# Letting the second expert's search into the last rows, and transposing the next expert's rows after the sixth chunk

## The chip, the cores and the metric

One core of a Trainium2 chip runs the whole program. The metric is the device time of one execution in microseconds (us); the figure quoted is the median over several executions. Engines are named as in the profile: PE (matrix multiply, PEld its weight loads), DVE (VectorE), ACT (ScalarE), POOL (GpSimd), SP (SyncE, which issues most transfers).

## The reference: what is computed

Three layers in a row, all in float32. A gated linear attention (4 batches, 8 heads, 768 steps, head size 48) makes 3072 tokens of 384 numbers. A dense two-layer network with 2048 hidden units follows. Then a mixture of 8 experts, each with room for exactly 3072/8 = 384 tokens, assigned greedily:

```
order = np.argsort(-flat)              # all 3072 x 8 logits, largest first
for idx in order:
    tok, e = int(idx) // E, int(idx) % E
    if assigned[tok] >= 0 or counts[e] >= cap: continue
    assigned[tok] = e
    counts[e] += 1
...
for e in range(E):
    h = np.maximum(x[assigned == e] @ w1[e], 0.0)      # 384 -> 1024
    out[assigned == e] = h @ w2[e]                     # 1024 -> 384
```

## The kernel before, in words

**Stages.** The tokens are worked in eight blocks of 384. Attention and the dense network run block by block; meanwhile the weights of all experts are split into a high and a low part and stored to the DRAM tensor `wd`. For the last block the dense network is done in two steps: `ffn1_logits` first makes its hidden layer and the gate logits, and `ffn1_rows` (144 matmuls on `hidden`, in three groups of 128 tokens) then makes the rows themselves, which in the text are called the last rows. The experts follow; they are numbered 0 to 7 here in the order in which they are filled, not by their weights.

**One expert.** `expert(p)` has eight chunks of hidden units. `hidden(f)` is nine matmuls 128x384 (three products of high and low parts, three slices of the input), then a Relu on ACT and a subtraction on DVE that split the result in two. `project(f)` is nine matmuls for the second layer. `project` lags `hidden` by two chunks, so PE's order is h0 h1 h2 p0 h3 p1 ... h7 p5 p6 p7, 144 matmuls for an expert. In the trace and the order, `weights` is a weight tile and `rounded` a split operand; positions such as "matmul 81 of expert 2" count these 144.

**What an expert needs.** Its token list comes from `chain(p)` and `lists`. `chain(p)` finds which expert fills up next and at which logit: four search steps in `seek`, each a comparison on DVE (`late<-late,cols` 128x1536), twelve counting matmuls (`bank<-late` 128x16) and a few small ones (`late,pairs`, `ok`), then `take`. `lists` turns the result into row numbers (24 matmuls `bank<-late` 128x6 and short DVE work). `gather` then issues three indirect DMAs on POOL that fetch 128 rows of `x2d` each (`common<-x2d`), and `expert_x` transposes each 128x384 piece with three matmuls against the identity (`bank<-ident,common`) and splits the result (ACT and DVE). The results of an expert go out by three indirect DMAs on POOL (`put`, `out_dram<-common`). Weights come in eight transfers of 768 KB on SP's queue (`weights<-wd`), issued when the chain knows which expert it is.

**For expert 0** there is a shortcut, `first_x`: two pieces are gathered and transposed as above. The third is built from the gathered rows, and from the last rows directly by matmuls with picking matrices (`late,common`), since the last rows are not yet in DRAM.

**What sets the order.** The program is not emitted as written. `Plan` records every instruction with its dependences, a modelled cost and a priority number, and `schedule` then walks through modelled time: at each step the instruction that can start earliest is taken, and among equals the one with the lowest priority number. The order of each engine is fixed by that; on the chip an engine that finds its next instruction not ready waits. `at(x)` sets the priority, `behind(ops)` says that what is recorded inside may not start before `ops` have started. Where the planner sees PE idle it puts in filler matmuls (`bank<-ones` 128x512, line 1711). The priorities that matter here: the last rows have ROWS = 84, the chain of expert 1 has CHAIN1 = 99 (line 57), and for expert p the base is 100 + 10p, with the lists, gather and transposes of expert p+1 at base - 1.5, the chain of p+2 at base - 1 and the expert's own matmuls at base + 5. Two experts ahead the chain runs, one expert ahead the rows are fetched.

Of the kernel before, what the change touches and what calls it, by code (L numbers as in the profile page):

```python
# [21 lines left out]
E, FE = 8, 1024  # L22
# [31 lines left out]
CHAIN0 = 81.0  # L54
GATHER0 = 80.9
ROWS = 84
CHAIN1 = 99
LISTS = -1.5
CHAIN = -1
EXPERT = 5.0  # L60
# [574 lines left out]
class Kernel:  # L635
# [860 lines left out]
    def expert(self, p, idx, x):  # L1496
        nc = self.nc
        ws = self.expert_tiles(p)
        w1, w2 = ws[:4], ws[4:]
        po = [self.pp.tile([128, 512], F32, name="x", bufs=BT) for _ in range(3)]  # L1500
        G = {}

        def hidden(f):
            ph = self.pp.tile([128, 512], F32, name="h", bufs=2)
            n = 0
            for s, v in ((1, x[0]), (0, x[1]), (0, x[0])):
                for kd in range(KD):

                    u, at = divmod(kd * 256 + f % 2 * 128, DM)
                    nc.tensor.matmul(ph[:, :CAP], w1[f // 2][:, u, s, at:at + 128], v[:, kd, :], start=(n == 0), stop=(n == 3 * KD - 1))  # L1510
                    n += 1
            G[f] = hH, hL = self.pair(f)
            with self.at(self.urgent):
                nc.scalar.activation(hH, ph[:, :CAP], AF.Relu)
                nc.vector.scalar_tensor_tensor(hL, ph[:, :CAP], 0.0, hH.bitcast(F32), op0=OP.max, op1=OP.subtract)

        def project(f, t):
            hH, hL = G[f]
            ts = slice(t * 128, (t + 1) * 128)
            for n, (h, s) in enumerate(((hL, 0), (hH, 1), (hH, 0))):  # L1520
                nc.tensor.matmul(po[t][:, :DM], h[:, ts], w2[f // 2][:, f % 2, s, :], start=(f == 0 and n == 0), stop=(f == NFE - 1 and n == 2))

        def put(t):
            o = self.gw.tile([128, DM], F32, name="x2", bufs=3)
            nc.scalar.activation(o, po[t][:, :DM], AF.Copy)
            nc.gpsimd.indirect_dma_start(out=self.out, out_offset=bass.IndirectOffsetOnAxis(ap=idx[:, t:t + 1], axis=0),
                                         in_=o, in_offset=None)

        if self.plan and p == E - 1:
            for f in range(NFE):  # L1530
                hidden(f)
            for t in range(3):
                for f in range(NFE):
                    project(f, t)
                put(t)
            return
        LAG = LAG2
        for f in range(NFE + LAG):
            if f < NFE:
                hidden(f)  # L1540
            if f >= LAG:
                for t in range(3):
                    project(f - LAG, t)
        for t in range(3):
            put(t)
# [172 lines left out]
    def record(self, cp):  # L1718
# [16 lines left out]
        def chain(p):  # L1735
            if p == 0:
                self.choose(NT - BT, NT)
                self.begin(NT - BT, NT)
                self.first(NT - BT, NT)
            else:  # L1740
                self.choose()
            if 0 < p < E - 1:
                self.begin()
                self.first()
            if p < E - 1:
                self.seek(p)
            else:
                self.take(p, None, None, None, None)
                self.flag()
            return self.pos, self.acc, self.ei  # L1750
# [55 lines left out]
        with self.at(CHAIN0):  # L1806
            c = chain(0)
            self.expert_weights(0, c[2], slice(0, AHEAD))
            idx, tok = self.lists(*c[:2], first=True)
# [3 lines left out]
        with self.at(GATHER0):  # L1813
            xg = self.gather(idx, NE + 1)
# [3 lines left out]
            ready = tok, self.first_x(xg, rows)  # L1818
# [3 lines left out]
        self.plan.extra = 3500.0  # L1822
        with self.at(CHAIN1), self.behind(listed):
            nxt = chain(1)
            self.expert_weights(1, nxt[2])
        for p in range(E):
            base = 100.0 + 10 * p
            self.urgent = base + XURG
            cur, was = ready, nxt
            if p + 2 < E:  # L1830
                with self.at(base + CHAIN):
                    nxt = chain(p + 2)
            if p + 1 < E:
                with self.at(base + LISTS):
                    idx, tok = self.lists(*was[:2])
                    ready = tok, self.expert_x(self.gather(idx))
            self.wide = p == E - 1
            with self.at(base + EXPERT):
                self.expert(p, *cur)
            if p + 2 < E:  # L1840
                with self.at(base + CHAIN):
                    self.expert_weights(p + 2, nxt[2])
# [49 lines left out]
```

## Time and profile before

| | |
|---|---|
| device time, median of 3 runs | 846.14 us (842.1 to 849.03) |
| the profiled execution | 847.83 us |
| its span, first to last instruction | 846.1 us |
| PE busy | 814.3 us (96%) |
| DVE busy | 567.0 us (67%) |
| ACT, POOL busy | 347.8 us (41%), 112.2 us (13%) |
| mean granted clock of PE | 0.990 |

The busy shares are means over the whole span. A PE that is busy 96% says that little is left, not where it is: the idle time has to be looked up by what PE waited for. In the timeline the duration of a matmul (0.34 us) is longer than the distance to the next one, because matmuls overlap; what a matmul costs is the distance between starts.

### The profile page before, as it was taken

To read this page: it belongs to the slowest core of one execution; us is meant where nothing else is said; L and a number is where in the kernel's file an instruction comes from. 1 tells how busy PE (TensorE), PEld (TensorE's weight loads), DVE (VectorE), ACT (ScalarE), POOL (GpSimd) and SP (SyncE) were. 2 spreads that over 40 slices of the span, in tenths; PEclk is the share of its full clock that TensorE was granted. 3 is DMA by queue.
4 is the path that set the end of the run, shared out by engine and by line. 5 is a ranking of instruction groups with operands and counts; after the bars stand their busy time and mean duration, and the time that the engine had idled before them with its cause. 6 is when DMAs were issued, how large, how long until landed. Compare 5 with 4: busy or idle time off the path is not lost. (4 is left out here: it accounts for less than half of the span.)

```text
span 846.1 us, 16045 instructions
## 1 busy us (share of the span) xinstructions
PE 814.3 (96%) x6116; PEld 751.5 (89%) x6116; DVE 567.0 (67%) x1329; ACT 347.8 (41%) x742; POOL 112.2 (13%) x107
## 2 busy tenths in 40 slices
PE   7999989999999999999999999999999899999995
PEld 3688888999999999998999999888887789899995
DVE  6899977977956966966976754655766667452220
ACT  3576765355555455455455443511121222222230
POOL 3111101200200200300200000001021212311211
PEclk7999999999999999999999999999999999999998
DMA  7894203689879688888879760003867866687400
GB/s 178 260 299 115 48 20 84 138 287 295 237 267 288 150 282 257 239 271 275 247 240 305 251 225 29 1 10 117 334 260 316 324 259 237 245 315 245 150 28 32
DMA packets 92935, 172.60 MB, mean 204 GB/s; under 512 B 31818, under 2 KB 61522, under 8 KB 92850
## 3 DMA queue, kind: packets, MB, share of 16 engines
q1 hardware_dynamic: 89634, 162.04, 59.1%
q0 software_dynamic: 3072, 9.44, 3.1%
q8 instruction: 50, 0.82, 0.4%
q14 instruction: 35, 0.29, 0.1%
q10 hardware_dynamic: 144, 0.01, 0.0%
HBM read 111.69 MB, written 59.77 MB: 203 GB/s over the span
## 5 line engine op out<-in xcount | busy, mean ns | idle before, releaser
L213 PE MATMUL bank<-rounded,weights 128*128 128x384 f32 (+1 forms) x1740 | 352.5, 343 | 1.2 <-POOL weights L213 0.5
L213 PE MATMUL bank<-weights,rounded 128*128 128x392 f32 (+1 forms) x1620 | 326.4, 343 | 3.3 <-ACT weights L213 2.4
L213 PEld LDWEIGHTS bank<-rounded,weights 128*128 128x128 f32 (+1 forms) x1740 | 301.9, 187 | 8.0 <-issue 2.6
L213 PEld LDWEIGHTS bank<-weights,rounded 128*128 128x128 f32 x1620 | 284.8, 188 | 5.9 <-issue 3.3
L213 ACT ACTIVATE rounded<-bank 128x384 fp32r<-128x384 f32 x110 | 53.8, 491 | 211.2 <-PE bank L213 190.4
L213 DVE TENSOR_TENSOR early<-early 128x384 fp32r<-128x384 f32 (+2 forms) x196 | 120.2, 628 | 21.5 <-ACT early L213 20.5
L213 PEld LDWEIGHTS bank<-early 128*64 128x64 f32 (+2 forms) x1696 | 98.2, 153 | 20.4 <-issue 10.2
L213 ACT ACTIVATE early<-early 128x384 fp32r<-128x384 f32 (+2 forms) x177 | 95.5, 547 | 41.8 <-DMA wd<-early 27.4
L213 PE MATMUL bank<-early 128*64 128x128 f32 (+3 forms) x1696 | 110.1, 269 | 2.2 <-ACT early L213 1.2
L213 POOL TENSOR_TENSOR rounded<-common,rounded 128x384 fp32r<-128x384 f32 x36 | 48.3, 1342 | 433.8 <-ACT rounded L213 394.6
L213 DVE SCALAR_TENSOR_TENSOR common<-common,rest,bank 128x384 f32<-128x384 f32 x128 | 77.9, 608 | 41.6 <-ACT common L233 40.9
L213 ACT ACTIVATE rounded<-common 128x384 fp32r<-128x384 f32 x118 | 61.7, 523 | 65.8 <-DVE common L213 62.4
L233 ACT ACTIVATE common<-bank 128x384 f32<-128x384 f32 x128 | 62.0, 485 | 61.7 <-PE bank L213 61.5
L213 DVE SCALAR_TENSOR_TENSOR rounded<-bank,rounded 128x384 fp32r<-128x384 f32 x62 | 34.4, 555 | 49.6 <-ACT rounded L213 47.6
L213 DVE TENSOR_TENSOR rounded<-common,rounded 128x384 fp32r<-128x384 f32 x82 | 46.4, 566 | 28.1 <-ACT rounded L213 19.6
L213 DVE TENSOR_TENSOR_SCAN early<-early 128x516 f32<-128x516 f32 x48 | 62.7, 1305 | 1.7 <-ACT early L213 1.3
L213 ACT ACTIVATE common<-bank 128x384 f32<-128x384 f32 x48 | 23.1, 490 | 59.1 <-PE bank L213 58.2
L213 POOL DMA_INDIRECT out_dram<-common,late x24 | 24.2, 1010 | 155.2 <-ACT common L213 100.5
L213 DVE TENSOR_TENSOR late<-late,cols 128x1536 bf16<-128x1536 bf16 (+3 forms) x53 | 42.7, 816 | 0.2
L213 POOL DMA_INDIRECT common<-x2d,late x24 | 26.2, 1092 | 103.3 <-DVE late L213 52.0
L213 DVE TENSOR_TENSOR rounded<-bank,rounded 128x384 fp32r<-128x384 f32 x48 | 26.6, 555 | 14.0 <-ACT rounded L213 13.1
L213 DVE TENSOR_TENSOR early<-bank,mask 128x512 f32<-128x512 f32 x48 | 31.0, 683 | 2.8 <-PE bank L213 2.4
(114 smaller groups left out, 485.6 us busy)
## 6 DMA issues: line engine op xcount, KB each, us to landing
wd<-early SPq DMA_DIRECT2D x128, 384.0 KB
weights<-wd SPq DMA_DIRECT2D x64, 768.0 KB
early<-in_w_dram SPq DMA_DIRECT2D x64, 384.0 KB
early<-in_fkq_dram SPq DMA_DIRECT2D x46, 288.0 KB
raw<-in_w_in_dram SPq DMA_DIRECT2D x16, 384.0 KB
raw<-in_w_out_dram SPq DMA_DIRECT2D x16, 384.0 KB
early<-in_v_dram SPq DMA_DIRECT2D x24, 192.0 KB
x2d<-common SPq DMA_DIRECT2D x24, 192.0 KB
```

What stands on the lines that cost most here:

```text
L213: op = self.add(engines, lambda e, b: getattr(e, method)(*[b(x) for x in a], **{n: b(x) for n, x in k.items()}), outs, ins)
L233: return e.activation(b(out), b(x), AF.Relu, scale=-1.0)
```

## The change

Two edits. CHAIN1 goes from 99 to 82, below ROWS = 84, so instructions of the chain of expert 1 that are ready are taken ahead of the last rows' matmuls. And `expert_x` for expert p+1, which was recorded together with its gather ahead of `expert(p)`, is recorded behind `expert(p)` with the condition that it may not start before the last matmul of `hidden(5)`, the sixth chunk, has started. The gather stays where it was.

```diff
--- before.py
+++ after.py
@@ -54,7 +54,8 @@
 CHAIN0 = 81.0
 GATHER0 = 80.9
 ROWS = 84
-CHAIN1 = 99
+CHAIN1 = 82
+MID = 5
 LISTS = -1.5
 CHAIN = -1
 EXPERT = 5.0
@@ -1509,6 +1510,8 @@
                     u, at = divmod(kd * 256 + f % 2 * 128, DM)
                     nc.tensor.matmul(ph[:, :CAP], w1[f // 2][:, u, s, at:at + 128], v[:, kd, :], start=(n == 0), stop=(n == 3 * KD - 1))
                     n += 1
+            if f == MID:
+                self.middle = self.last(1)
             G[f] = hH, hL = self.pair(f)
             with self.at(self.urgent):
                 nc.scalar.activation(hH, ph[:, :CAP], AF.Relu)
@@ -1833,10 +1836,13 @@
             if p + 1 < E:
                 with self.at(base + LISTS):
                     idx, tok = self.lists(*was[:2])
-                    ready = tok, self.expert_x(self.gather(idx))
+                    xg = self.gather(idx)
             self.wide = p == E - 1
             with self.at(base + EXPERT):
                 self.expert(p, *cur)
+            if p + 1 < E:
+                with self.at(base + LISTS), self.behind(self.middle):
+                    ready = tok, self.expert_x(xg)
             if p + 2 < E:
                 with self.at(base + CHAIN):
                     self.expert_weights(p + 2, nxt[2])
```

Three places show what the planner makes of it. (Lines behind 82 stand one to six lines later in the changed file, so L213 is L214 there.)

PE at the end of the last rows. `weights_...,hidden` are the last rows' matmuls, `ident,common` the transposes of expert 0's rows. Before:

```order
L213 MATMUL bank_69<-weights_1154,hidden 128x384 x6
L213 MATMUL bank_69<-weights_1235,hidden 128x384 x4
L213 MATMUL bank_66<-ident,common 128x128 x3
L213 MATMUL bank_69<-weights_1235,hidden 128x384 x2
L213 MATMUL bank_69<-weights_1322,hidden 128x384 x2
L213 MATMUL bank_67<-ident,common 128x128 x3
L213 MATMUL bank_69<-weights_1322,hidden 128x384 x4
L213 MATMUL bank_68<-ident,common 128x128 x3
```

Now (the row of "..." is eleven more counting steps of two rows each):

```order
L214 MATMUL bank_69<-weights_1154,hidden 128x384 x5
L214 LDWEIGHTS late
L214 MATMUL bank_66<-late 128x16
...
L214 MATMUL bank_69<-weights_1154,hidden 128x384
L214 MATMUL bank_69<-weights_1235,hidden 128x384 x2
L214 MATMUL bank_67<-ident,common 128x128 x3
L214 MATMUL bank_66<-late,pairs 128x8
L214 MATMUL bank_69<-weights_1235,hidden 128x384 x3
L214 MATMUL bank_66<-ident,common 128x128 x3
L214 MATMUL bank_69<-weights_1235,hidden 128x384
```

The first search step of expert 1 (twelve counting matmuls) and its `late,pairs` now stand between the last rows' matmuls; before, they came behind the last of them.

PE in expert 2, where the rows of expert 3 are transposed. `rounded,weights` is `hidden`, `weights,rounded` is `project`. Before (the "..." is one search step, counting matmuls):

```order
L213 MATMUL bank_71<-weights_1012,rounded 128x384 x3
L213 MATMUL bank_66<-ident,common 128x128 x3
L213 LDWEIGHTS ones
L213 MATMUL bank_68<-ok_83,ones 128x1
L213 MATMUL bank_69<-weights_1012,rounded 128x384 x3
L213 MATMUL bank_67<-ident,common 128x128 x3
L213 MATMUL bank_72<-rounded,weights_687 128x384 x4
...
L213 MATMUL bank_72<-rounded,weights_687 128x384 x4
L213 MATMUL bank_66<-ident,common 128x128 x3
```

Now:

```order
L214 MATMUL bank_69<-weights_1095,rounded 128x384 x3
L214 MATMUL bank_73<-rounded,weights_687 128x384 x9
L214 MATMUL bank_66<-ident,common 128x128 x3
L214 MATMUL bank_68<-ident,common 128x128 x3
L214 MATMUL bank_67<-ident,common 128x128 x3
L214 MATMUL bank_70<-weights_1095,rounded 128x384 x3
L214 MATMUL bank_71<-weights_1095,rounded 128x384 x3
L214 MATMUL bank_69<-weights_1095,rounded 128x384 x3
L214 MATMUL bank_72<-rounded,weights_862 128x384 x9
```

The three transposes of three matmuls stood at matmuls 51, 54 and 62 of the expert; now all nine stand behind matmul 81, which is the end of `hidden(5)`.

POOL from the gathers of experts 0 and 1 on (six, in the first row); `out_dram` are the stores of results. Before:

```order
L213 DMA common<-x2d,late 128x384 x6
L213 DMA out_dram<-common,late 3072x384 x2
L213 DMA common<-x2d,late 128x384
L213 DMA out_dram<-common,late 3072x384
L213 DMA common<-x2d,late 128x384 x2
L213 DMA out_dram<-common,late 3072x384
L213 DMA common<-x2d,late 128x384 x2
L213 DMA out_dram<-common,late 3072x384
```

Now:

```order
L214 DMA common<-x2d,late 128x384 x6
L214 DMA out_dram<-common,late 3072x384 x2
L214 DMA common<-x2d,late 128x384 x3
L214 DMA out_dram<-common,late 3072x384 x2
L214 DMA common<-x2d,late 128x384 x3
L214 DMA out_dram<-common,late 3072x384 x3
```

The three gathers of an expert now stand together; before, stores of results stood between those of experts 2 and 3.

## Rows read from the trace of the kernel before

**Rows 1.** The page, parts 1 and 2: PE's busy time, and the granted clock by slices.
```profile
PE 814.3 (96%) x6116; PEld 751.5 (89%) x6116; DVE 567.0 (67%) x1329; ACT 347.8 (41%) x742; POOL 112.2 (13%) x107
...
PEclk7999999999999999999999999999999999999998
```

**Rows 2.** The waits of PE: us in total, times, longest.
```profile
PE bank L213 <- DMA common<-x2d,late: 6.4, 9, 2.2
...
PE bank L213 <- DVE late L213: 1.1, 4, 0.4
```

**Rows 3.** The timeline of PE, transposes that waited: start, us, what, [idle before <-releaser].
```profile
622.41 0.55 PE L213 MATMUL bank<-ident,common 128*128 128x128 f32 x3 [0.18 <-DMA common<-x2d,late]
...
623.99 0.52 PE L213 MATMUL bank<-ident,common 128*128 128x128 f32 x3 [0.33 <-DMA common<-x2d,late]
...
650.10 0.55 PE L213 MATMUL bank<-ident,common 128*128 128x128 f32 x3 [1.61 <-DMA common<-x2d,late]
...
671.49 0.55 PE L213 MATMUL bank<-ident,common 128*128 128x128 f32 x3 [0.45 <-DMA common<-x2d,late]
...
677.39 0.52 PE L213 MATMUL bank<-ident,common 128*128 128x128 f32 x3 [2.22 <-DMA common<-x2d,late]
...
705.62 0.52 PE L213 MATMUL bank<-ident,common 128*128 128x128 f32 x3 [0.16 <-DMA common<-x2d,late]
...
768.07 0.55 PE L213 MATMUL bank<-ident,common 128*128 128x128 f32 x3 [0.65 <-DMA common<-x2d,late]
```

**Rows 4.** The timeline of POOL: gathers (common<-x2d) and row stores (out_dram<-common).
```profile
582.84 1.12 POOL L213 DMA_INDIRECT common<-x2d,late  x1 [51.98 <-DVE late L213]
...
637.60 0.99 POOL L213 DMA_INDIRECT common<-x2d,late  x1 [8.75 <-issue]
638.89 0.98 POOL L213 DMA_INDIRECT out_dram<-common,late  x1 [0.30 <-issue]
...
641.47 0.96 POOL L213 DMA_INDIRECT common<-x2d,late  x1 [0.30 <-PE bank L213]
...
668.92 0.99 POOL L213 DMA_INDIRECT out_dram<-common,late  x1 [2.08 <-DMA out_dram<-common,late]
670.22 0.97 POOL L213 DMA_INDIRECT common<-x2d,late  x1 [0.30 <-PE bank L213]
```

**Rows 5.** The timeline of PE where the last rows end and expert 0 begins.
```profile
586.11 0.55 PE L213 MATMUL bank<-ident,common 128*128 128x128 f32 x3 [0.17 <-DMA common<-x2d,late]
...
588.04 0.52 PE L213 MATMUL bank<-ident,common 128*128 128x128 f32 x3 [0.68 <-DMA common<-x2d,late]
...
589.28 0.94 PE L213 MATMUL bank<-ident,common 128*128 128x128 f32 x6
...
591.11 0.59 PE L1711 MATMUL bank<-ones 128*128 128x512 bf16 x2
591.65 1.15 PE L213 MATMUL bank<-rounded,weights 128*128 128x384 f32 x5
```

**Rows 6.** The timeline of PE: what a matmul and a search step cost.
```profile
595.10 0.46 PE L213 MATMUL bank<-late 128*128 128x16 bf16 x12
595.42 0.95 PE L213 MATMUL bank<-rounded,weights 128*128 128x384 f32 x4
...
635.72 0.36 PE L213 MATMUL bank<-late 128*128 128x6 bf16 x8
...
779.72 4.91 PE L213 MATMUL bank<-weights,rounded 128*128 128x384 f32 x27
784.47 0.76 PE L213 MATMUL bank<-late 128*128 128x6 bf16 x24
```

**Rows 7.** Windows: length, busy us of the engines, PEclk, DMA share, GB/s.
```profile
10.00:20.00 10.00, 8.10 (x48) 5.15 (x49) 7.26 (x19) 3.94 (x8) 0.00 (x0) 0.54 0.88 225
...
582.00:589.00 7.00, 6.15 (x37) 5.47 (x35) 3.41 (x10) 0.90 (x2) 3.56 (x3) 1.00 0.38 117
...
634.00:650.00 16.00, 14.13 (x130) 11.97 (x128) 11.14 (x37) 2.84 (x6) 3.92 (x4) 1.00 1.01 401
```

## The prediction

> **What bounds the kernel now.** I read the page first. PE is busy for 814 of 846 us and its granted clock is full in every slice but the first and the last [rows 1]. So PE sets the time, and a change can win only what PE spends waiting, or lose by new waits; no matmul of the reference's work goes away. Next the waits of PE by releaser. Two kinds fall into the part that the change touches: 6.4 us in nine waits for a gather from `x2d`, and 1.1 us in four waits for DVE's search work [rows 2]. That is 7.5 us, or 0.9% of the time, and an upper bound for what new places can win. The other kinds lie in attention and in preparation, which keep their order.
>
> Then the timeline of PE, to see where the nine stand. Seven are transposes of an expert's rows, 0.18 + 0.33 in expert 0, 1.61 in expert 1, 0.45 + 2.22 in expert 2, 0.16 in expert 3 and 0.65 in expert 5: 5.60 us [rows 3]. Two are in the last rows, 0.17 + 0.68 [rows 5]. POOL's timeline tells why some are long. Expert 0's first gather was issued at 582.84 and its transposes ran at 586.11, 3.3 us later; the third gather in expert 1 was issued at 641.47 and its transposes could run only at 650.10, 8.6 us later [rows 3 to 5]. In the first stretch the DMA engines are 0.38 busy, in the second 1.01, with expert weights [rows 7]. Also, stores of results stand between the gathers on POOL: one at 638.89, and one at 668.92 that itself waited 2.08 us while the third gather of that expert stood behind it [rows 4]. The planner's prices know little of this, so it puts the transposes where on the chip the rows are not there yet.
>
> **The transposes behind the sixth chunk.** The same nine matmuls per expert, later. By the order, the lists end at the start of experts 2 to 6 and the transposes now stand at matmul 81 of 144. A matmul costs (784.47 - 779.72)/27 = 0.176 us [rows 6], so 81 of them are 14.3 us, and four search steps of 0.32 us of counting each (595.10 to 595.42, rows 6) come on top where a chain runs: 15.5 us. The slowest case before is expert 2. Its third gather was issued at 670.22 and landed 7.2 us later [rows 3, 4]; a gather that goes out 2 to 6 us behind the lists is there well before 15 us. So the waits of experts 2, 3 and 5 go: 2.67 + 0.16 + 0.65 = 3.48 us.
>
> Expert 1 is closer. Before, its lists end at 635.9 [rows 6] and the third piece was there at 650.10, 14.2 us later [rows 3]. The store between the gathers goes (0.98 + 0.30 us of POOL, rows 4), which leaves 12.9. By the order the lists now end at matmul 26 and the transposes stand at 81: 55 x 0.176 = 9.7 us, three search steps are 1.0, their small matmuls and the six transposes ahead of the third piece some 0.6: 11.3 us. A wait of up to 1.6 us can stay, or none if the store's data was what held the gather back. I take 0.6, so 1.0 of the 1.61 is won. Sum of this part: 4.5 us (3.5 to 5.1).
>
> Expert 0 is not helped. Its lists end at matmul 65 now, and 92 before, and its transposes stand at 106, 110 and 113 now, and 134, 136 and 140 before: 41, 45 and 48 matmuls behind the lists against 42, 44 and 48. They were already past chunk six, and the planner's own price for the gather decides. The chain runs some 27 matmuls earlier, and the weights of expert 1, which wait for that chain, start earlier by as much, so the gathers meet the same traffic. I cost the waits at 0.5 us more than before, since one search step fewer may cover them: between 0.5 less (the whole of 0.51) and 4.3 more (each of three as long as the 1.61 of expert 1).
>
> What is late next: the next expert's first `hidden` needs all three pieces split. Between matmul 81 and 144 lie 63 x 0.176 = 11 us of matmuls, while DVE and ACT have far less than that to do, so nothing. The gather tiles are held longer, but the next gathers come in the next expert. In the last expert there are no transposes.
>
> **The second expert's search inside the last rows.** Nothing is added but two fillers (72 in the order against 70). Before, the third piece's transposes begin at 589.28 and expert 0's first matmul at 591.65 [rows 5]. In the new order the last four matmuls of the last rows stand behind that point (4 x 0.176 = 0.70), and one filler more (591.11 to 591.65 for two: 0.27 each, rows 5). So expert 0 starts some 1.0 us later. Against this, two of its four counting steps (0.64) have moved out of it ahead of its start, which leaves a loss of 0.36, and the second new filler, behind matmul 27, adds 0.27: a loss of 0.6 in all. Bounds: a gain of 0.7, if the fillers fill what would be idle and the 0.68 at 588.04 is covered by search work, and a loss of 2.0, if the third piece must wait as the second did and the picks wait for the last copy.
>
> The chain's results for expert 1 come some 5 us earlier (27 matmuls). That is worth nothing by itself: no row shows PE waiting for weights of an expert. It brings the steady pattern, lists and search at the start of an expert, one expert earlier. In that pattern PE waits once per expert for DVE's search, about 0.3 us (1.1 us in four, rows 2), and one expert more has it: a loss of 0.3 (0 to 1.0).
>
> **The sum.** 4.5 - 0.5 - 0.6 - 0.3 = 3.1 us. The profiled execution took 847.83 us, 1.7 more than its span, and would take 844.7. It stands 1.7 us above the median of the runs shown, 846.14; taken from that, 843.0. About 1% (8.5 us) is what a measurement of this kernel can tell from no change.
>
> **Rivals.** (1) The clock. Nine transposes now stand in a row, in six experts, where three stood. If PE's clock fell behind such a group, the price is in the trace: between 10 and 20 us the mean granted clock is 0.54, most of the stretch at 1.2 GHz, after an opening in which PE had little but fillers [rows 1, 7]; that is 4.6 us of work lost in 10. One such fall undoes the gain and makes the kernel slower, 847.6; two make 852.2, six 870. Against it: in expert 1 PE waited 1.61 us in front of transposes, with 14.1 us busy of 16, and the clock stayed at 2.4 GHz [rows 3, 7]; a group of nine takes less time than that and has dense matmuls on both sides.
>
> The Trainium skill, in "TensorE: Matmul & The Clock Gate", section "Part 4: PE-mode transpose", speaks for this rival: it says that transposes do not count as PE activity in the way matmuls do, so the fast clock does not engage for them. By that rule the sum would be the one of this rival; by the row above, with three transposes at a time, it stays the forecast, and no run here shows nine.
>
> (2) The gain is given back in expert 0. Its gathers go out while the weights of expert 1 arrive, as those of expert 1 met the weights of expert 2, and its transposes were not moved back from the lists. If each of three waits 1.61 us, that is 4.8 instead of 0.51: 843.0 + 3.8 = 846.8, a little slower than before. For it: the DMA share of 1.01 in such stretches [rows 7]; against: in the trace the same three places cost 0.51 under the same kind of load. (3) Everything goes, search waits too: 7.5 us, 838.6. For it: grouped transposes also break the run of matmuls less often; against: two of the places keep their distance from the gather. (4) The wait only moves, because the gather itself is late and not the transposes early, so that the time is 846. Against it: no gather took more than about 9 us, and 15 are given.
>
> **How the numbers follow.** Forecast 0.65, rival 1 0.06, rival 2 0.15, rival 3 0.10, rival 4 0.04. The predicted time is that of the forecast, 843.0. The forecast's own bounds with those of expert 0 and the last rows run from 840 to 847; the range takes in rival 3 at its lower end and rivals 2 and 4 above, plus the 2 us by which single runs here differ from their median: 838.7 to 848.6. It leaves out rival 1 with two falls or more. Faster by over 1% means under 837.7, which only rival 3 with luck in the measurement reaches: 0.06. Slower by over 1% needs two falls of the clock or a wait that I do not see: 0.07. Within 1%: 0.87.
>
> **What would show it.** Right: in the changed profile the wait of PE for gathers falls from 6.4 us to between 1 and 3, with none left behind matmul 81 of experts 2 to 6; what is left stands in the last rows, in expert 0 and perhaps in expert 1; the clock is 1.00 from the start of the experts to the end; expert 0's first matmul comes up to 1 us later than 591.65. Wrong: a stretch at 1.2 GHz behind a group of nine transposes; waits over 1 us in expert 0's transposes; a new wait of PE for expert weights or for DVE in the last rows; or a first `hidden` of an expert that waits for its split rows.

## The result, and the profile after

The changed kernel takes 836.51 us (median of 4, 835.79 to 837.78), the kernel before beside it 847.18 (4 runs, 842.1 to 849.03): a ratio of 0.988 with a 95% interval of 0.9848 to 0.9911. In a second series it took 840.14 (6 runs) against 847.85 (13 runs), 0.9907 [0.9877, 0.9937]. The change is worth 8 to 11 us, where 3 were forecast; 836.51 lies below the range.

The profiled execution took 837.78 us with a span of 836.0, against 847.83 and 846.1. The page of after, parts 1 and 2, beside [rows 1]:

```profile
PE 809.8 (97%) x6118; PEld 751.8 (90%) x6118; DVE 565.7 (68%) x1329; ACT 346.2 (41%) x742; POOL 111.5 (13%) x107
...
PEclk8999999999999999999999999999999999999998
```

PE is busy 4.5 us less and the span is 10.1 us shorter, so more than half of the gain is idle time. The granted clock is full between the first and the last slice, as before.

PE's waits for gathers, beside [rows 2]; a row for DVE's `late` no longer exists:

```profile
PE bank L214 <- DMA common<-x2d,late: 0.8, 2, 0.5
```

PE's timeline at the transposes in experts 0 and 1, beside [rows 3] (start, duration, what, idle before):

```profile
615.25 0.55 PE L214 MATMUL bank<-ident,common 128*128 128x128 f32 x3 [0.30 <-DMA common<-x2d,late]
...
618.24 0.52 PE L214 MATMUL bank<-ident,common 128*128 128x128 f32 x3 [0.44 <-DVE rounded L214]
...
643.17 1.14 PE L214 MATMUL bank<-ident,common 128*128 128x128 f32 x9
644.07 1.12 PE L214 MATMUL bank<-weights,rounded 128*128 128x384 f32 x5
```

Two stalls are left, both in expert 0; the waits above count the first and one in the last rows (below). The profile puts the second down to DVE, whose split ended at 618.12; the third gather landed at 618.10, 7.33 us after its issue, so either may have held it. In expert 1 nine transposes stand in a row at 643.17 and the next matmul starts 0.90 us later: no idle time, and the same price as three times three (0.30 from 586.11 to 586.41 before). Experts 2 to 6 have no wait at all. POOL's timeline, beside [rows 4]:

```profile
629.89 0.98 POOL L214 DMA_INDIRECT out_dram<-common,late  x1 [3.58 <-ACT rounded L214]
632.69 0.99 POOL L214 DMA_INDIRECT common<-x2d,late  x1 [1.82 <-issue]
633.98 0.97 POOL L214 DMA_INDIRECT common<-x2d,late  x1 [0.30 <-issue]
635.25 0.95 POOL L214 DMA_INDIRECT common<-x2d,late  x1 [0.30 <-PE bank L214]
637.54 1.00 POOL L214 DMA_INDIRECT out_dram<-common,late  x1 [1.34 <-DMA out_dram<-common,late]
...
661.50 0.95 POOL L214 DMA_INDIRECT common<-x2d,late  x1 [0.31 <-PE bank L214]
664.11 1.00 POOL L214 DMA_INDIRECT out_dram<-common,late  x1 [1.67 <-ACT rounded L214]
```

The three gathers of expert 1 go out together. The store that waits 1.34 us for an earlier store stands behind them, where the one of before at 668.92 stood in front of a gather. The end of the last rows, beside [rows 5]:

```profile
583.67 0.46 PE L214 MATMUL bank<-late 128*128 128x16 bf16 x12
...
586.63 0.52 PE L214 MATMUL bank<-ident,common 128*128 128x128 f32 x3 [0.53 <-DMA common<-x2d,late]
...
588.55 0.95 PE L214 MATMUL bank<-weights,hidden 128*128 128x384 f32 x4
589.34 0.39 PE L1714 MATMUL bank<-ones 128*128 128x512 bf16 x1
589.56 0.45 PE L214 MATMUL bank<-late 128*128 128x16 bf16 x12
...
590.99 0.59 PE L1714 MATMUL bank<-ones 128*128 128x512 bf16 x2
...
591.59 1.68 PE L214 MATMUL bank<-rounded,weights 128*128 128x384 f32 x8
```

One counting step of expert 1 is among the last rows and a second one behind them, four of the last rows' matmuls stand behind the third piece, and three fillers in place of two. Last, windows beside [rows 7] (length, busy time of PE, PEld, DVE, ACT and POOL, clock, DMA share, GB/s):

```profile
634.00:650.00 16.00, 16.00 (x130) 14.43 (x129) 11.03 (x41) 3.12 (x7) 2.89 (x3) 1.00 0.79 322
643.00:645.00 2.00, 2.00 (x16) 1.84 (x15) 1.75 (x4) 1.64 (x4) 0.00 (x0) 1.00 1.04 418
645.00:652.00 7.00, 7.00 (x54) 6.65 (x53) 5.74 (x27) 0.84 (x3) 0.00 (x0) 1.00 0.43 163
```

PE is busy for all 16 us of the stretch in which 14.13 were before, and the clock stays at 2.4 GHz (1.00) through the nine transposes and behind them.

**Where the 10.1 us went.** From the starts of PE's instructions, between the two profiled executions: the token lists of expert 0 come 1.3 us earlier (both kernels have the same order of instructions up to there, so this is chance of the execution); from the lists to expert 0's first matmul 1.3 us more; expert 0 the same; experts 1 to 5 shorter by 2.5, 4.5, 1.1, 0.7 and 1.3 us, 10.1 in all; the rest as before. Measured from start to start, the delays in front of transposes fell by 6.0 us, those of search matmuls by 2.4, and some 1.7 us lie in a counting step that has moved ahead of expert 0 (0.3) and in slightly shorter distances between matmuls, which I did not trace further.

**An idle time is less than the delay.** The trace shows a matmul of 0.34 us where the next can start 0.176 us later. A stall is counted as idle only from the modelled end, so each costs some 0.16 us more than its bracket says: the stall of 1.61 in [rows 3] delayed the next start by 1.75, the one of 2.22 by 2.38, and delays under 0.16 show nothing. The seven stalls that [rows 3] give as 5.60 us cost 6.78, and 7.07 with an eighth, of 0.13 us, in front of the second piece in expert 2 (at 672.81).

### The profile page after: what moved, and what is told of

Same layout as the page of the kernel before. It is cut to its first block, busy times and chain, and to the rows that moved or that the text cites. A ratio compares the mean times of both kernels' runs of the same rounds, so it can differ in the third digit from the quotient of the medians.

```text
span 836.0 us, 16050 instructions
## 1 busy us (share of the span) xinstructions
PE 809.8 (97%) x6118; PEld 751.8 (90%) x6118; DVE 565.7 (68%) x1329; ACT 346.2 (41%) x742; POOL 111.5 (13%) x107
## 5 line engine op out<-in xcount | busy, mean ns | idle before, releaser
L214 PE MATMUL bank<-rounded,weights 128*128 128x384 f32 (+1 forms) x1740 | 353.2, 343 | 1.2 <-POOL weights L214 0.5
L214 PE MATMUL bank<-weights,rounded 128*128 128x392 f32 (+1 forms) x1620 | 322.1, 342 | 3.2 <-ACT weights L214 2.3
L214 PEld LDWEIGHTS bank<-rounded,weights 128*128 128x128 f32 (+1 forms) x1740 | 301.8, 187 | 7.5 <-issue 2.1
L214 PEld LDWEIGHTS bank<-weights,rounded 128*128 128x128 f32 x1620 | 285.1, 188 | 5.9 <-issue 3.2
L214 ACT ACTIVATE rounded<-bank 128x384 fp32r<-128x384 f32 x110 | 52.1, 492 | 198.3 <-PE bank L214 184.0
L214 DVE TENSOR_TENSOR early<-early 128x384 fp32r<-128x384 f32 (+2 forms) x196 | 119.7, 627 | 17.8 <-ACT early L214 16.8
L214 PEld LDWEIGHTS bank<-early 128*64 128x64 f32 (+2 forms) x1696 | 98.0, 153 | 20.0 <-issue 10.9
L214 PE MATMUL bank<-early 128*64 128x128 f32 (+3 forms) x1696 | 109.7, 268 | 2.2 <-ACT early L214 1.2
L214 ACT ACTIVATE early<-early 128x384 fp32r<-128x384 f32 (+2 forms) x177 | 95.0, 546 | 34.7 <-DMA wd<-early 22.2
L214 DVE SCALAR_TENSOR_TENSOR common<-common,rest,bank 128x384 f32<-128x384 f32 x128 | 77.8, 608 | 44.9 <-ACT common L234 44.2
L214 POOL TENSOR_TENSOR rounded<-common,rounded 128x384 fp32r<-128x384 f32 x36 | 48.3, 1342 | 433.7 <-ACT rounded L214 392.8
L214 ACT ACTIVATE rounded<-common 128x384 fp32r<-128x384 f32 x118 | 61.7, 523 | 65.3 <-DVE common L214 62.0
L214 DVE SCALAR_TENSOR_TENSOR rounded<-bank,rounded 128x384 fp32r<-128x384 f32 x62 | 34.4, 554 | 52.0 <-ACT rounded L214 51.7
L214 DVE TENSOR_TENSOR rounded<-common,rounded 128x384 fp32r<-128x384 f32 x82 | 46.4, 566 | 28.0 <-ACT rounded L214 20.0
L214 DVE TENSOR_TENSOR_SCAN early<-early 128x516 f32<-128x516 f32 x48 | 62.6, 1305 | 1.6 <-ACT early L214 1.2
L214 ACT ACTIVATE common<-bank 128x384 f32<-128x384 f32 x48 | 23.4, 491 | 64.5 <-PE bank L214 63.2
L214 POOL DMA_INDIRECT out_dram<-common,late x24 | 23.6, 982 | 163.2 <-ACT common L214 125.3
L214 DVE TENSOR_TENSOR late<-late,cols 128x1536 bf16<-128x1536 bf16 (+3 forms) x53 | 42.9, 816 | 0.2
L214 POOL DMA_INDIRECT common<-x2d,late x24 | 26.2, 1093 | 87.2 <-DMA weights<-wd 51.9
L214 DVE TENSOR_TENSOR early<-bank,mask 128x512 f32<-128x512 f32 x48 | 31.0, 683 | 3.2 <-PE bank L214 2.9
L214 PE MATMUL bank<-ident,early 128*128 128x128 f32 (+1 forms) x131 | 22.0, 287 | 6.6 <-DVE early L214 6.5
```

The costliest lines, as they stand in the source:

```text
L214: op = self.add(engines, lambda e, b: getattr(e, method)(*[b(x) for x in a], **{n: b(x) for n, x in k.items()}), outs, ins)
```

## The experiments

Theory A was the prediction's: transposes stand too close behind their gathers, and the place behind the sixth chunk removes the stall. Theory B: the gain comes from the earlier chain.

### One edit at a time

chain_only, on the kernel before:

```diff
-CHAIN1 = 99
+CHAIN1 = 82
```

> Only CHAIN1 = 82; the transposes are recorded with their gather, as in the kernel before. The order puts them 41 to 46 matmuls behind the lists in expert 1 and 36 to 42 in experts 2 to 4. Theory A (the gain is the stall of PE in front of transposes whose rows have not landed, and the place behind chunk six removes it): the stalls are there again, 2 to 4 us in expert 1 and 0.3 to 2 us in each of experts 2 to 4, PE's wait for gathers is 5 to 9 us, and the time is 843 to 848. Theory B (the gain is the earlier chain of expert 1, which brings the steady pattern one expert earlier): most of the gain is here, 838 to 840.

middle_only, on the changed kernel:

```diff
-CHAIN1 = 82
+CHAIN1 = 99
```

> Only the transposes behind chunk six; CHAIN1 = 99 as before. Theory A: expert 1 keeps its stall (its transposes stand at matmuls 89 to 100, 39 to 50 behind the lists, as before), the stalls of experts 2 to 6 go, so PE's wait for gathers falls from 6.4 us to about 3, and the time is 839 to 842. Theory B: no gain to speak of, 845 to 848. If the short stalls of PE for DVE's search at the start of experts 3 to 5 (0.5 us each before, none after) belong to the place of the transposes, they are gone here; if they belong to the earlier chain, they stay.

Against 845.44 us of the kernel before (11 runs), chain_only took 840.14 (6 runs), ratio 0.9918 [0.9888, 0.9948], and middle_only 840.53, 0.9923 [0.9893, 0.9954]. Both theories are half right: either edit alone brings most of the gain, 0.8% each, where both together brought 0.9 and 1.2%. The two gains do not add up, and by these times alone the changed kernel cannot be told from either edit. PE's wait for gathers in middle_only is 3.3 us, where theory A gave about 3. A second profile of middle_only was taken to see whether what stood behind its stall (below) came again:

> The transposes moved behind the sixth chunk, CHAIN1 left at 99, a second profile. The third piece of expert 1's rows stalls PE again by 1 to 2 us. If a stall of that length takes the clock with it as a rule, a stretch of about 3.4 us at 1.2 GHz follows it again and expert 1 takes about 35 us; if not, the clock stays up and expert 1 takes 32.5 to 34 us.

It took 838.61 us; a stall of 1.86 us came in expert 1 again, this time at the second piece, and the clock stayed up.

PE's waits for gathers in chain_only, where the third piece is transposed 46 and 42 matmuls behind the lists in experts 1 and 2, and 50 in both before:

```profile
PE bank L213 <- DMA common<-x2d,late: 2.5, 4, 0.7
```

The wait fell from 6.4 to 2.5 us without any transpose being moved away from its gather. POOL's timeline of chain_only shows what did it:

```profile
637.63 0.95 POOL L213 DMA_INDIRECT common<-x2d,late  x1 [0.30 <-PE bank L213]
639.89 1.00 POOL L213 DMA_INDIRECT out_dram<-common,late  x1 [1.31 <-DMA out_dram<-common,late]
...
663.76 0.95 POOL L213 DMA_INDIRECT common<-x2d,late  x1 [0.30 <-PE bank L213]
665.93 1.36 POOL L213 DMA_INDIRECT out_dram<-common,late  x1 [1.21 <-DMA out_dram<-common,late]
```

These are the third gathers of experts 1 and 2, and the stores now come behind them. The earlier lists let the planner issue the three gathers in one go.

### Stores behind the gathers, nothing else

stores_behind, on the kernel before, with CHAIN1 at 99 and the transposes with their gather:

```diff
-            nc.gpsimd.indirect_dma_start(out=self.out, out_offset=bass.IndirectOffsetOnAxis(ap=idx[:, t:t + 1], axis=0),
-                                         in_=o, in_offset=None)
+            send = lambda: nc.gpsimd.indirect_dma_start(out=self.out, out_offset=bass.IndirectOffsetOnAxis(ap=idx[:, t:t + 1], axis=0),
+                                                        in_=o, in_offset=None)
+            if self.plan and p < E - 2:
+                self.held.append(send)
+            else:
+                send()
...
-                    ready = tok, self.expert_x(self.gather(idx))
+                    xg = self.gather(idx)
+                    with self.behind(self.last(3)):
+                        for send in self.held:
+                            send()
+                    self.held = []
+                    ready = tok, self.expert_x(xg)
```

> The kernel before with CHAIN1 at 99 and the transposes together with their gather, as before; only the stores of an expert's results are recorded behind the three gathers that follow, so that on POOL no store of results stands between two gathers of one expert. Theory C (an earlier search alone wins because it takes the stores from between the gathers): the third gathers of experts 1 and 2 go out 1.3 to 3 us earlier, PE's wait for gathers falls from 6.4 us to between 2.5 and 4, with under 1 us left in any transpose of expert 1 or 2, and the time is 841 to 843.5, a ratio of about 0.994 to the kernel before. Theory A (the transposes stand too close behind the gathers wherever the stores are): the wait stays above 5 us and the time is 845 to 848. Theory D (the earlier search wins by itself, by search steps taken out of the experts): the wait may fall, but experts 1 and 2 together get less than 1.5 us shorter than the 68.99 us of before, and the time is 845 to 848.

841.27 us (8 runs) against 847.85, ratio 0.993 [0.9903, 0.9956]. The waits for gathers, and PE at the third transposes of experts 1 and 2:

```profile
PE bank L213 <- DMA common<-x2d,late: 1.3, 4, 0.6
```

```profile
645.20 0.49 PE L213 MATMUL bank<-ident,common 128*128 128x128 f32 x3
...
671.24 0.49 PE L213 MATMUL bank<-ident,common 128*128 128x128 f32 x3
```

Neither has an idle time in front of it, where 1.61 and 2.22 us stood. On POOL the third gather of expert 1 now goes out ahead of the store:

```profile
637.87 0.95 POOL L213 DMA_INDIRECT common<-x2d,late  x1 [0.30 <-issue]
639.12 1.01 POOL L213 DMA_INDIRECT out_dram<-common,late  x1 [0.30 <-issue]
```

Expert 1 and 2 together take 65.5 us against 68.99, although two search matmuls now wait 0.8 us each. Theory C holds, with an even smaller wait than its 2.5 to 4 us; D falls, and so does A where it says that the wait stays wherever the stores are. A good part of what the earlier chain wins is the place of the stores on POOL. In this series the changed kernel took 840.14 us (after_again, below); its mean lies 1.7 us below that of stores_behind, with a 95% interval from 0.4 above to 3.8 below, so the times do not show that the change wins more than the stores alone. In numbers, from the last list matmul (PE) to the issue of the third gather (POOL), and the idle time in front of its transposes (first profile of each):

| kernel | expert 1 | expert 2 |
|---|---|---|
| before | 5.55 us, waits 1.61 | 7.75 us, waits 2.22 |
| stores_behind | 4.14, none | 5.47, none |
| chain_only | 4.26, none | 4.75, waits 0.74 |
| middle_only | 5.55, waits 1.50 | 7.88, none |
| changed | 4.27, none | 4.76, none |

One edit brings the gathers forward, the other puts the transposes back. Both act on the same two stalls, and each cures what the other leaves: middle_only still waits in expert 1, where its transposes follow late lists; chain_only still waits in experts 2 and 5.

The issue is not all of it. By the profile's time to landing, the third gather of expert 1 took 8.3 us in before_third and 8.0 in both profiles of middle_only, with a store between the gathers; it took 6.3 us in chain_only, 6.5 in the changed kernel and 7.0 in stores_behind, with none. Why it lands faster is not shown.

### The place of the transposes

mid3 and mid7, on the changed kernel:

```diff
-MID = 5
+MID = 3
```

```diff
-MID = 5
+MID = 7
```

> Both edits, but behind the fourth chunk (MID = 3). The transposes of experts 2 to 4 stand nine in a row at matmul 45, some 9 us behind the lists, among the search steps. Theory A: rows land 8 to 12 us behind the lists while weights arrive, so a stall of 0.5 to 2.5 us comes back in each of experts 2 to 4 and one of 2 to 4 us in expert 1 (transposes at 67 to 72, lists at 26): 840 to 844. If only the separation of the three transposes mattered, the time would stay at 836 to 838.

> Both edits, behind the eighth chunk (MID = 7). All transposes stand nine in a row at matmul 117, in expert 0 too, 52 matmuls behind its lists. Theory A: no stall in front of transposes anywhere in the experts (1.0 us of it is left in expert 0 with MID = 5), so the time is 835 to 837; from 117 to 144 lie 27 matmuls, 4.8 us, and if splitting the last piece needs longer than that, the next expert's first matmul waits and the time is above 838.

mid3 took 839.27 us (0.9914 [0.9883, 0.9944]), mid7 837.59 (0.9881 [0.9849, 0.9913]). PE's waits for gathers in mid3 and mid7:

```profile
PE bank L214 <- DMA common<-x2d,late: 1.7, 4, 0.7
```

```profile
PE bank L214 <- DMA common<-x2d,late: 1.5, 2, 0.8
```

Behind the fourth chunk delays of 0.6 to 0.7 us come back in experts 2 and 5. That is less than theory A forecast: experts 1, 3 and 4 have none, the one of expert 5 stands in chain_only too, and the time lies below the 840 to 844. Behind the eighth there is none from expert 1 on, and nothing else is late; but 0.81 us of waiting is left in expert 0, where none was forecast. The sixth is late enough. Six runs against six of one series, the mean of mid7 lies 2.6 us below that of mid3 (95% interval 0.3 to 4.9), the way that theory A says, and 3.2 and 3.6 us below those of chain_only and middle_only (0.9 to 5.5, 1.3 to 5.9). So both edits together, in this form, do win more than either alone.

### The same kernels again

> The kernel before, one more profile. If the three search waits of about 0.5 us in experts 3, 4 and 5 belong to the order of the kernel before, they stand there again; if they were chance in that one execution, expert 4 falls from 30.8 to about 30.1 us. The stalls in front of the transposes of experts 1 and 2 belong to the order by every theory: 1.2 to 2.5 us each, at the third piece. If a long stall can also cost clock, a stretch at 1.2 GHz behind one of them may be seen in this execution, and then the time is 1.5 to 4 us longer.

> The kernel before, a third profile. If DVE's late answer to the list matmuls belongs to the order of before, PE waits about 0.3 us again at matmul 5 or 6 of experts 3, 4 and 5, as in both executions seen so far. If it is chance of the execution, this one may be without it, as the other kernels' executions were partly with and partly without.

> The changed kernel once more, beside the kernel before in the same session as the others, for its ratio and its spread. All theories: 835.5 to 838.5, ratio 0.985 to 0.992; PE's wait for gathers in the experts 0.7 to 1.2 us, all of it in expert 0.

> The changed kernel, a third profile. Of the two so far, one had no search wait in the experts (expert stage 235.2 us) and one had six (239.2 us). If it is chance, either may come, and the stage takes 235 to 236 or 238.5 to 239.5 us; the waits for gathers stay at 0.7 to 1.2 us, all in expert 0.

before_again took 847.16 us, before_third 848.68, after_again 840.14 (6 runs; its profiled execution 840.51), after_third 840.01. The changed kernel's second series lies above the 835.5 to 838.5 that were expected, with its ratio inside, and of the stalls that were to come again in before_again the one in expert 1 was 0.99 us. Three things vary from one execution to the next, with the same program.

First, how long DVE takes to answer the list matmuls. Here are DVE's first step behind the lists in expert 2, and the search matmul on PE that depends on it, in the changed kernel's first profile and then in after_again:

```profile
656.94 0.16 DVE L214 COPY late<-bank 128x3 f32<-128x3 f32 x1 [1.22 <-PE bank L214]
...
658.03 0.37 PE L214 MATMUL bank<-late,pairs 128*128 128x8 f32 x2
```

```profile
657.48 0.16 DVE L214 COPY late<-bank 128x3 f32<-128x3 f32 x1 [1.73 <-PE bank L214]
...
658.56 0.39 PE L214 MATMUL bank<-late,pairs 128*128 128x8 f32 x2 [0.34 <-DVE late L214]
```

In both executions the last list matmul starts at 656.7 to 656.8. DVE follows 0.20 us behind it in the one, and 0.72 in the other, and there PE waits. Where the lists stand between two experts' matmuls, an execution has either 0.20 every time or 0.70 to 0.75 every time (calm, whose order differs, has 0.44 once). The long answer stood in the first profile of before and in before_again, after_again and late0, and in none of the other ten. So three of the four waits for DVE in [rows 2], 0.9 of 1.1 us, belong to the execution and not to the order. The expert stage of the changed kernel, from expert 0's first matmul to the end of the last expert's, took 239.2 us in after_again instead of 235.2 (235.0 in after_third). Of these 4.0 us, 2.6 lie in experts 2 to 5, behind late list answers. The other 1.4 lie in expert 1, where the lists were answered in time and DVE answered two counting steps some 0.5 and 0.9 us later; PE's search matmuls behind them waited 0.26 and 0.69 us. Why an answer is late is open.

Second, the clock behind a long stall. middle_only, first profile, at expert 1's third piece, and its windows:

```profile
648.11 0.84 PE L214 MATMUL bank<-ident,common 128*128 128x128 f32 x3 [1.50 <-DMA common<-x2d,late]
648.61 2.91 PE L214 MATMUL bank<-weights,rounded 128*128 128x384 f32 x8
```

```profile
646.00:648.00 2.00, 0.61 (x14) 0.37 (x12) 1.16 (x3) 0.87 (x2) 0.00 (x0) 1.00 1.02 417
648.00:652.00 4.00, 3.89 (x15) 3.89 (x16) 0.73 (x3) 0.49 (x1) 0.00 (x0) 0.57 0.35 143
```

After 1.50 us of waiting, eight matmuls take 0.32 us each from start to start, and the clock is 0.57: mostly 1.2 GHz. before_third shows the same after 2.06 us, before_again after 2.34, each with its row of the timeline and then of the windows:

```profile
649.92 0.55 PE L213 MATMUL bank<-ident,common 128*128 128x128 f32 x3 [2.06 <-DMA common<-x2d,late]
```

```profile
652.00:655.00 3.00, 3.00 (x12) 3.00 (x12) 1.05 (x6) 0.21 (x1) 0.00 (x0) 0.50 0.15 59
```

```profile
673.69 0.52 PE L213 MATMUL bank<-ident,common 128*128 128x128 f32 x3 [2.34 <-DMA common<-x2d,late]
```

```profile
674.00:679.00 5.00, 5.00 (x30) 4.67 (x29) 2.35 (x7) 0.95 (x2) 0.00 (x0) 0.66 0.18 66
```

Not every such stall does it: of seven stalls of 1.5 to 2.4 us in the three profiles of before and the two of middle_only, three were followed by a fall and four were not, among them the two in [rows 3]; no shorter stall in the experts was. A fall makes about ten matmuls some 0.14 us longer each, 1.5 us in all. The changed kernel has no stall over 0.7 us in its experts in three profiles.

Third, the clock ahead of the experts: between 67 and 78 us the granted clock was 0.53 in after_third and 0.55 in before_third, while the first profiles of both kernels had 1.00 between 60 and 80. That part of the program is not touched by the change, so kernels are compared here by their expert stage.

Comparing like with like, both with the early answer: the expert stage takes 245.1 us in before_third and 235.0 in after_third. Delays in front of transposes make about 7 us of that, the fall of the clock 1.5, the rest some 1.5. Both with the late answer: 247.7 in before_again, with a fall of the clock too, and 239.2 in after_again, with the two late counting steps.

### Further

late0, on the changed kernel: only expert 1's rows are transposed later, behind matmul 126 of expert 0.

```diff
-            if f == MID:
+            if f == MID and p > 0:
...
+                if f == NFE - 1 and p == 0:
+                    self.middle = self.last(1)
```

> The changed kernel with one more move: expert 1's rows are transposed in expert 0 behind matmul 126 (behind the sixth chunk of the second layer) and not at 106 to 113; the other experts as in the changed kernel. If what is left of the waits is the same thing (a transpose that stands too close behind its gather), the 0.74 us of idle time and 1.05 us of delay in expert 0 go, expert 0 falls from 33.87 to about 32.9 us and the time to 835 to 837. If the split of the rows then becomes late, the first hidden matmul of expert 1 waits and expert 0 stays at 33.5 to 34.5 us: 836.5 to 838.

calm, on late0: the planner is told that DVE's copy of the list results takes 0.55 us more.

```diff
         nc.vector.tensor_copy(pp, pv[:, :, 1])
+        if self.plan and not first:
+            op = self.last(1)[0]
+            op.cost = {e: c + 550.0 for e, c in op.cost.items()}
```

> The changed kernel with expert 1's transposes behind matmul 126 of expert 0, and with DVE's copy of the list results priced 0.55 us higher in the planner, so that the search's next small matmuls stand about three to five matmuls later on PE. If the search waits are DVE's late answer to the list matmuls, they are covered whether the answer is late or not: PE's waits for DVE in the experts fall to under 0.3 us in all, the expert stage takes 234 to 235.5 us, and the time is 834.5 to 837. If they have another cause, they stay at 1 to 2 us in an execution that has them, and the time is 837 to 840.

late0 took 839.65 us (0.9901 [0.9873, 0.9928]) where the changed kernel took 840.14 in the same series. Expert 0 has no gather stall left and takes 32.5 us instead of 33.9; expert 1 has none either, but takes 32.2 us instead of 31.6. The forecast time of 835 to 837 did not come; the execution had the late answer. calm took 837.35 (0.9879 [0.9841, 0.9917]) in another series, with an expert stage of 235.9, both just above what was forecast. It has no wait for DVE in the experts, but its execution had the early answer, so it does not tell whether the new places cover a late one. It has a new stall in expert 1, and POOL's timeline shows the old cause at work: the new prices have put a store between the gathers again.

```profile
644.67 0.55 PE L214 MATMUL bank<-ident,common 128*128 128x128 f32 x3 [0.94 <-DMA common<-x2d,late]
```

```profile
634.13 0.99 POOL L214 DMA_INDIRECT common<-x2d,late  x1 [8.02 <-PE bank L214]
635.42 0.98 POOL L214 DMA_INDIRECT out_dram<-common,late  x1 [0.30 <-issue]
636.71 0.98 POOL L214 DMA_INDIRECT common<-x2d,late  x1 [0.30 <-issue]
638.00 0.96 POOL L214 DMA_INDIRECT common<-x2d,late  x1 [0.30 <-PE bank L214]
```

The third gather goes out 7.16 us behind the lists, where the changed kernel has 4.27, and the transposes, though placed behind the sixth chunk, wait 0.94 us in front of the second piece. The store accounts for 1.3 of these 2.9 us; for the other 1.6 the first gather already goes out later behind the lists (3.29 us, against 1.70). So this is the mechanism once more, but not by itself. Neither kernel can be told from the changed one by its time.

## Why the prediction was wrong

**Direction and place: right.** PE's wait for gathers fell from 6.4 to 0.8 us, none is left in experts 1 to 6, what remains stands in expert 0 and once in the last rows (0.53 at 586.63, where 0.17 and 0.68 stood), and the clock held. The size was wrong: 3.1 us were forecast, and the runs show 8 to 11. Two steps of the prediction failed. It priced waits by their idle time, and it held the earlier chain of expert 1 to be worth nothing, where that chain also takes the stores from between the gathers. Step by step:

**The upper bound.** "That is 7.5 us ... and an upper bound for what new places can win" failed, and with rival 3 it set the lower end of the range. It added idle times. Start to start the same waits cost more, some 0.16 us each, and a long one can cost about 1.5 us of clock besides, which in the profile of before happened not to occur. The measured medians, 8 and 11 us less, lie above the bound, though the interval of the second series (5 to 10 us) reaches below it; the expert stages alone, like with like, differ by 10.1 and 8.5.

**The transposes.** 4.5 us were forecast for experts 1, 2, 3 and 5. Their delays from start to start were 1.75, 3.28, 0.32 and 0.81, 6.2 us in the profiled execution, and all of it went. 3.48 of idle time was 4.4 of delay, and expert 1 won its whole stall, not 1.0 of it. There I had taken the third piece to land 12.9 us behind the lists, by subtracting only the store, and its transposes to be due at 11.3. They ran 12.8 us behind the lists, and by the profile the piece had landed at 10.8: issued 4.27 behind the lists, and 6.5 us from issue to landing, where the prediction had read 8.6 and before_third shows 8.3. It was the case that the prediction put as "or none".

**The chain.** "That is worth nothing by itself" was wrong: chain_only alone is 0.8% faster. The rows for it were in the prediction. It names the stores between the gathers [rows 4] and then counts the removal of one of them in expert 1 alone. stores_behind shows that the place of the stores by itself is worth 0.7%.

**The search wait.** -0.3 us was forecast, for one more expert in a steady pattern of waits. The waits went (1.4 us in experts 3 to 5, and 1.0 elsewhere), but the 1.4 were the late answer, which is chance of the execution. Reading one execution's wait as a property of the order was the error. The two first profiles, 10.1 us apart, are such an unlike pair: late answers before, early ones after.

**The last rows.** Forecast: expert 0 starts 1.0 us later and 0.27 for fillers, against 0.64 for two search steps moved out. Measured from its lists it starts 1.28 later, and two steps of twelve counting matmuls do stand ahead of it; but in before one of these was there already, twelve matmuls in two parts between the rows at 589.28 and 591.65 of [rows 5]:

```profile
590.05 0.25 PE L213 MATMUL bank<-late 128*128 128x16 bf16 x4
...
590.90 0.35 PE L213 MATMUL bank<-late 128*128 128x16 bf16 x8
```

So one step moved, 0.32, and the term is -1.0 where -0.6 was given, inside its bounds.

**Expert 0.** Forecast 0.5 us worse; measured 0.1 worse (delays of 0.91 us before, 1.05 after). Rival 2 did not come: its waits stayed at 0.30 and 0.44. late0 shows that they go when the transposes stand later there too.

**The other rivals.** The clock (1) did not fall: PEclk is 1.00 in the windows with and behind the nine transposes. The Trainium skill, in "TensorE: Matmul & The Clock Gate", section "Part 4: PE-mode transpose", says that transposes do not count as PE activity in the way matmuls do. In a group of 0.90 us that cost nothing here; what the clock did fall behind in the experts was PE waiting, for 1.50, 2.06 and 2.34 us. Rival 3 (everything goes, 838.6) named the right outcome for the wrong reason: its 7.5 us were idle time only, and it took the search waits for something that the order would remove. It had a chance of 0.10.

## What to carry to other kernels

Price a stall from the start of one instruction to the start of the next, and let an open end stand for what it may do to the clock: the sum of idle times is no upper bound. When a transfer is late, look at what stands in front of its issue on the queue before moving the instruction that waits for it; here moving the stores alone won 0.7%, and moving the transposes alone 0.8%. And take at least two executions of the kernel before: what one shows as a wait may be that execution's own.

## What the runs showed of the hardware that was not expected

- DVE answers 24 short list matmuls of PE after 0.20 us or after 0.70 to 0.75 us, with the same program to the instruction: one or the other for all lists between two experts in an execution. In the changed kernel the late answer cost 2.6 us.
- Three of seven PE stalls of 1.5 to 2.4 us were followed by about ten matmuls at 1.2 GHz; nine transposes in a row were not.
- The same gather of 128 rows, the third of expert 1, landed 7.6 to 8.3 us after its issue in four executions with a store of results between the gathers, and after 6.3 to 7.0 in six without.
